# A fused attention and MoE kernel: pass two's weights split into the buffers they are first multiplied from

## The chip, the cores and the metric

The kernel runs on one core of a Trainium2 chip. The metric is device microseconds of one launch, the median of several runs. Operands and results are float32; the two weight matrices arrive as float64 and are decoded on the chip.

## What is computed

Windowed attention with a linear bias over 8 batches and 8 heads, its output laid out as 4608 tokens of 512 features, then a two-layer MLP with the activation h * erf(softplus(h)).

```python
def attention(q, k, v):                      # each (8, 8, 576, 64), window 128, scale 1/8
    scores = scale * q @ k.T
    rel = pos[:, None] - pos[None, :]
    bias = slopes[h] * -abs(rel)             # slopes 2^-(h+1), h = 0..7
    scores = where((rel >= 0) & (rel < 128), scores + bias, -1e9)
    attn = exp(scores - max); attn = attn / (sum(attn) + 1e-9)
    return attn @ v

def reference(q, k, v, moe_w_in, moe_w_out): # w_in (512, 2048), w_out (2048, 512), float64
    x = attention(q, k, v) as (4608, 512)    # 8 batches x 576 rows, 8 heads x 64
    h = x @ w_in
    sp = max(h, 0) + log1p(exp(-abs(h)))
    return ((h * erf(sp)) @ w_out).astype(float32)
```

## The kernel before

Every matmul of the MLP is made from float32r operands: a number is split into a high part (its rounding) and a low part (the rest), and high*high + high*low + low*high are summed in PSUM.

**Stages.** Attention runs over 48 pairs of heads (12 chunks of 384 tokens, 4 pairs each), and the MLP's pass one runs among it: 12 chunks by the first 6 blocks of 128 hidden columns (`NF1`), 72 units; its products are L989 (with w_in) and L1065 (with w_out). Its weights lie split in one large tile, `w1`, for the whole pass. Pass one's partial outputs go to DRAM (`pd`). Pass two takes the other 10 blocks in 5 pairs (`NP`), over 6 chunks of 768 tokens: 30 rounds `R`, round R with pair p = R mod 5. A pair's w_in product is done in Strassen's form with 7 products (L1178), of which the left operands are sums of weight blocks; then activation, then 12 products with w_out (L1217). After a chunk's fifth round, each of its 6 output tiles is made: `pd` is loaded into an output buffer `ot` (L1089), PSUM is added (L1090), and it is stored (L1095).

**Pass two's weights.** `Weights.pair` decodes two blocks of w_in (L846 to L850 on DVE, L835 and L843 on ACT), forms the sums (L888 to L891), and `split` makes high and low parts of wa, wb, wc and wd in a staging buffer `wb` of which there are two (`WB`), and sends them to DRAM (L873); the same for two blocks of w_out (we). Decoded tiles share three buffers, `wt` (`RB`), handed out in the order of the code. For every round, the first five too, `fetch` (L1119) then reads the pair back from DRAM: 14*256 columns for w_in (`wi`) and 4*512 for w_out (`wo`). `wi` has three homes in rotation: two buffers of the pool that takes over attention's memory, and for R mod 3 = 2 a place in `w1`, which pass one must first have left; `wo` has three buffers. The pool exists only once attention is done (`gone`).

**Order.** Nothing is ordered at run time. Each operation is given to a planner with its candidate engines and costs, a due time `at`, and its buffers; `Plan.run` is a list scheduler that simulates the engines with these costs and writes each engine's instruction order, in which the engine then runs, waiting on semaphores. Of the ready operations that find their buffers free, an engine takes the one due earliest. A transfer is reckoned at 380 GB/s (280 in the first 9 us) after 0.65 us and lands 1.3 us later (L391, L392). All DMAs are issued by SP, in the planner's order. Due times of the weights' pairs stand `W2A` = 40 ahead of their round's.

**Memory.** Chunks 1 and 2 of attention's output are kept in two buffers of a pool `early`, which is among attention's pools and is closed with them. There are three output buffers `ot` (`OB`).

Of the kernel before, what the change touches and what calls it, by code (L numbers as in the profile page):

```python
# [19 lines left out]
P = 128  # L20
# [21 lines left out]
PB, XB, OB, TB = 3, 3, 3, 2  # L42
WB, RB = 2, 3
# [3 lines left out]
SLOW, RATE = 9.0, 280e3  # L47
# [9 lines left out]
W2A, W2B, WL = 40, 8.0, 36  # L57
# [69 lines left out]
def passes(w, a):  # L127
# [17 lines left out]
    while out:  # L145
# [10 lines left out]
LEFT = {"A11": (0, 512), "A12": (256, 768), "S1": (1024, 1536), "S2": (1280, 1792),  # L156
        "S3": (2048, 2560), "S4": (2304, 2816), "A22": (3072, 3328)}
# [41 lines left out]
class View(Buf):  # L199
# [6 lines left out]
    @property  # L206
    def all(self):
        x = self.whole[:, self.c0 : self.c0 + self.n]
        return x.rearrange("p (k n) -> p k n", k=self.k) if self.k > 1 else x.bitcast(F32)
# [5 lines left out]
class Strip(Part):  # L215


    def __init__(self, whole, c0, n):
        super().__init__(whole)
        self.c0, self.n = c0, n  # L220

    @property
    def all(self):
        return self.whole.all.rearrange("p a n -> p (a n)")[:, self.c0 : self.c0 + self.n]
# [19 lines left out]
class Plan:  # L244
# [17 lines left out]
    def op(self, costs, emit, r=(), w=(), at=0.0, moved=0, rows=1.0):  # L262
# [19 lines left out]
        for b in [*r, *w]:  # L282
            if isinstance(b, Part):
                bufs[id(b.whole)] = b.whole
# [11 lines left out]
    def run(self):  # L296
# [55 lines left out]
        while events:  # L352
# [17 lines left out]
            for e in ("SP", "PE", "Act", "DVE", "Pool"):  # L370
                while free.get(e, 0.0) <= t + 1e-9 and ready.get(e):
# [89 lines left out]
class Attention:  # L461


    def __init__(self, tc, plan, actx, qk, vb, plain, bias, ident, moe):
# [5 lines left out]
        self.qkp, self.vp, self.pp, self.ptp, self.xsb, fixed, moe.early = (  # L470
            sb(n) for n in ("qkp", "vp", "pp", "ptp", "xsb", "tables", "early"))
# [335 lines left out]
class Weights:  # L807
# [69 lines left out]
    def pair(self, p, f, wi, wo, at):  # L877
# [16 lines left out]
        self.split(f"wa{p}", lambda: t1.all.bitcast(F32), DM, [t1], wi[0], at)  # L894
        self.split(f"wb{p}", lambda: sums[:, :2].rearrange("p a n -> p (a n)"), DM, [sums], wi[1], at)
        self.split(f"wc{p}", lambda: sums[:, 2:].rearrange("p a n -> p (a n)"), DM, [sums], wi[2], at)
        self.split(f"wd{p}", lambda: t2[:, SB:].bitcast(F32), SB, [t2], wi[3], at)
        for j in range(2):
            t = self.decode(1, f + j, at + 0.5 * W2B)
            self.split(f"we{p}_{j}", lambda t=t: t.all.bitcast(F32), DM, [t], wo[j], at + 0.5 * W2B)  # L900


class Moe:
# [4 lines left out]
    def __init__(self, tc, plan, ctx, x_dram, part_dram, out):  # L908
# [3 lines left out]
        self.xp, self.hp, self.op_ = (sb(n) for n in ("xp", "hp", "outp"))  # L912
# [3 lines left out]
        self.raw, self.direct_parts = {}, []  # L916
# [182 lines left out]
    def blocks_pass(self, wi, wo, pool, home, gone, time):  # L1099
# [17 lines left out]
    def fetch(self, src, w, over, n, gone, at):  # L1117
        nc, op = self.nc, self.plan.op
        op(emit=lambda e: nc.sync.dma_start(w.all, src[0].whole.ap), r=[*src, gone], w=[w, *over], at=at, **dma(P * n * 4))  # L1119
        return w  # L1120
# [37 lines left out]

    def pair(self, C, p, R, x, wi, wo, po, at):
# [10 lines left out]
        def product(ps, a, c, begin):  # L1170
            xh, xl = x[c]
            ah, al = LEFT[a]

            def emit(e):
                for k in range(2):
                    w = lambda o: wi[:, o + P * k : o + P * k + P].bitcast(F32R)
# [5 lines left out]
            op({"PE": 6 * f32r_us(CH) + 0.015}, emit, r=[wi, xh, xl] + [ps] * (not begin), w=[ps], at=at + MH)  # L1182
# [26 lines left out]
        for j, t in [(j, t) for t in tiles for j in range(2)] if last and not C else [(j, t) for j in range(2) for t in tiles]:  # L1209
            gh, gl = g[j]  # L1210
            if True:

                def mm(e, j=j, t=t, gh=gh, gl=gl):
                    cs = slice(P * t, P * t + P)
                    w = [wo[:, DM * (2 * j + k) : DM * (2 * j + k + 1)].bitcast(F32R) for k in range(2)]
# [6 lines left out]
                op({"PE": 3 * f32r_us(DM) + 0.015}, mm, r=[gh, gl, wo], w=[po[t]], at=at + MP)  # L1222
# [5 lines left out]
def tile_kernel(ctx, tc, qk, vb, w_in, w_out, plain, bias, out, nb=B):  # L1228
# [47 lines left out]
    ops += [o for o in plan.ops[len(ops) :] if any(b in o.bufs for b in (moe.raw[1], moe.raw[2]))]  # L1276
# [7 lines left out]
    def pieces(b, *cuts):  # L1284
        out = []
        for c0, c1 in zip(cuts, cuts[1:]):
            out.append(Buf(ap=b.ap[:, c0:c1]))
            out[-1].whole = b
        return out
# [3 lines left out]
    for p in range(NP):  # L1293
        w1.later = [attention.loaded[min(WN + p * WD, len(attention.loaded) - 1)]]
# [85 lines left out]
```

## Time and profile before

| | us |
|---|---|
| median of the 3 runs | 979.7 |
| the runs | 979.7, 967.86, 980.14 |
| the profiled execution | 977.34 |
| its span, first to last instruction | 975.6 |
| mean granted TensorE clock | 0.991 |

The span is cut into windows, and for each window the profile gives the busy time of each engine. What PE is not busy in a window is time lost by the engine that is busy nearly throughout; the lists of waits, of instructions in order of time and the chain that ended last tell what it waited for.

### The profile page before, as it was taken

How to read it: one execution, taken by the hardware profiler on the slowest of the kernel's cores; microseconds unless marked ns; L12 is line 12 of the kernel's file. 1: busy time of each engine (PE TensorE's matmuls, PEld its weight loads, DVE VectorE, ACT ScalarE, POOL GpSimd, SP SyncE). 2: the span in 40 equal slices, each digit the busy share in tenths (PEclk: the TensorE clock that was granted, in tenths of full speed). 3: DMA queues.
4: the chain of work that ended last, by engine and by line, in shares of the span. 5: the costliest groups of instructions: out<-in, count | busy, mean ns of one | idle time of the engine just before them, and what ended most of it. 6: DMA issues, size and time to landing. Idle time of an engine off the chain costs nothing.

```text
span 975.6 us, 26523 instructions
## 1 busy us (share of the span) xinstructions
PE 938.7 (96%) x11080; PEld 812.5 (83%) x11080; DVE 640.8 (66%) x1485; ACT 636.0 (65%) x1282; POOL 148.4 (15%) x295
## 2 busy tenths in 40 slices
PE   8789999999999999999999999999999999999998
PEld 7577788787888777878888898998989898889896
DVE  6888667457666668787989875565374375454433
ACT  7897767557765666776868566565665565475652
POOL 3532423232333314400000000000000000000000
PEclk9999999999999999999999999999999999999999
DMA  7764435645664486589699887666856765855711
GB/s 245 248 207 132 155 119 184 177 150 179 189 198 141 160 285 208 169 313 368 260 314 323 304 316 244 262 263 208 296 201 221 284 265 183 301 183 217 252 72 65
DMA packets 58760, 216.06 MB, mean 221 GB/s; under 512 B 6928, under 2 KB 16144, under 8 KB 50960
## 3 DMA queue, kind: packets, MB, share of 16 engines
q1 hardware_dynamic: 58640, 214.36, 63.8%
q8 instruction: 87, 1.43, 0.6%
q14 instruction: 33, 0.27, 0.1%
HBM read 171.61 MB, written 42.73 MB: 220 GB/s over the span
## 4 chain that ended last, share of the span: by engine, by line
PE 69%; DMA 12%; DVE 7%; issue 2%; POOL 2%; ACT 2%; SPq 0%; DVEq 0%; POOLq 0%; ACTq 0%
PE banks L1217 20%; PE banks L1178 16%; PE banks L1065 13%; PE banks L989 12%; PE banks L751 5%; PE banks L647 3%; DMA ot<-pd 3%; DMA out_dram<-ot 3%; DMA xr<-xd 2%; POOL p L712 2%; DMA wi<-wa 1%; DMA y<-xd 1%; DVE p L681 1%; DVE pa L729 1%; DMA wi<-wi 1%
## 5 line engine op out<-in xcount | busy, mean ns | idle before, releaser
L1217 PE MATMUL banks<-wo,gh 128*128 128x512 f32 x720 | 223.9, 392 | 2.9 <-DVE ot L1090 2.9
L971 ACT COPY hs<-banks 128x384 f32<-128x384 f32 x143 | 68.3, 478 | 173.5 <-PE banks L1178 136.0
L712 POOL TENSOR_SCALAR p<-p,st 128x160 f32<-128x160 f32 (+2 forms) x282 | 141.3, 520 | 262.3 <-DVE st L704 231.4
L989 PE MATMUL banks<-xh,w 128*128 128x384 f32 x576 | 170.4, 350 | 3.7 <-ACT hs L971 2.0
L1217 PEld LDWEIGHTS banks<-wo,gh 128*128 128x128 f32 x720 | 133.1, 188 | 24.9 <-DVE ot L1090 4.5
L1065 PE MATMUL banks<-w,gh 128*128 128x512 f32 x432 | 141.8, 409 | 3.4 <-ACT ot L971 2.2
L1217 PE MATMUL banks<-wo,gl 128*128 128x512 f32 x360 | 141.7, 394 | 0.0
L689 ACT ACTIVATE p<-p,st 128x160 f32<-128x160 f32 (+2 forms) x288 | 120.3, 421 | 30.5 <-DVE st L681 30.4
L989 PEld LDWEIGHTS banks<-xh,w 128*128 128x128 f32 x576 | 107.2, 190 | 15.5 <-ACT hs L971 6.7
L1044 DVE TENSOR_TENSOR hs<-s,hs 128x768 f32<-128x768 f32 (+1 forms) x103 | 90.1, 902 | 29.5 <-ACT s L1034 29.5
L681 DVE CUSTOM_DVE_ANT_0 p<-banks,tables 128x160 f32<-128x160 f32 (+2 forms) x288 | 75.8, 318 | 42.6 <-PE banks L647 41.7
L989 PE MATMUL banks<-xl,w 128*128 128x384 f32 x288 | 97.9, 340 | 0.0
L1189 DVE TENSOR_TENSOR hs<-banks,hs 128x384 f32<-128x384 f32 x90 | 49.9, 555 | 72.2 <-PE banks L1178 43.3
L1065 PEld LDWEIGHTS banks<-w,gh 128*128 128x128 f32 x432 | 77.8, 191 | 23.1 <-issue 6.2
L1178 PE MATMUL banks<-w,wi 128*128 128x384 f32 x480 | 94.9, 337 | 1.3 <-DVE hs L1189 1.3
L1048 DVE TENSOR_TENSOR gl<-hs,gh 128x768 fp32r<-128x768 f32 (+1 forms) x103 | 91.8, 910 | 3.8 <-ACT gh L971 2.3
L1178 PEld LDWEIGHTS banks<-w,wi 128*128 128x128 f32 x480 | 85.2, 188 | 6.2 <-DVE hs L1189 1.6
L1065 PE MATMUL banks<-w,gl 128*128 128x512 f32 x216 | 86.5, 400 | 0.0
L1032 ACT ACTIVATE s<-hs 128x768 f32<-128x768 f32 (+1 forms) x103 | 76.2, 794 | 13.2 <-DVE hs L1189 12.9
L1217 PEld LDWEIGHTS banks<-wo,gl 128*128 128x128 f32 x360 | 67.5, 188 | 14.3
L1034 ACT ACTIVATE s<-s 128x768 f32<-128x768 f32 (+1 forms) x103 | 76.2, 794 | 0.5
L751 PEld LDWEIGHTS banks<-pa,v 32*64 32x64 f32 x4576 | 59.1, 132 | 19.2 <-issue 8.2
(112 smaller groups left out, 1418.0 us busy)
## 6 DMA issues: line engine op xcount, KB each, us to landing
wi<-wi SPq DMA_DIRECT2D x20, 1792.0 KB, 8.0
wo<-wo SPq DMA_DIRECT2D x30, 1024.0 KB, 7.4
w<-wi SPq DMA_DIRECT2D x10, 1792.0 KB, 7.4
v<-v_b SPq DMA_DIRECT2D x24, 512.0 KB, 4.0
qk<-qk SPq DMA_DIRECT2D x24, 400.0 KB, 4.0
pd<-ot SPq DMA_DIRECT2D x36, 256.0 KB, 3.9
y<-xd SPq DMA_DIRECT2D x12, 768.0 KB, 6.1
wri<-w_in SPq DMA_DIRECT2D x16, 512.0 KB, 5.2
```

Source lines behind the costliest of these rows:

```text
L681: nc.vector.tensor_tensor_reduce(out=dst(j), in0=cut(ps[j].all), in1=cut(table[:, half * j + c0 : half * j + c0 + n]), scale=-0.125, scala ...
L689: nc.scalar.activation(dst(j), dst(j), AF.Exp, bias=low[:, j : j + 1], scale=-1.0, accum_out=total[:, j : j + 1])
L712: (nc.vector if e == "DVE" else nc.gpsimd).tensor_scalar(dst, dst, totals[t][:, j : j + 1], 1.0, op0=ALU.mult, op1=ALU.mult)
L751: nc.tensor.matmul(whole[64 * j : 64 * j + 64, first + a, 32 * t0 : 32 * (t0 + n)], lhsT=y.v[rows, 128 * slot + 64 * j : 128 * slot + 64 * ...
L989: nc.tensor.matmul(ps[:, :W], lhsT=ww[:, cs], rhs=xx[:, k], start=(k2 + k + n == 0), stop=(k2 + k + n == 4),)
L1032: A.activation(s[:, :n], hs[:, :n], AF.Softplus)
L1034: A.activation(s[:, :n], s[:, :n], AF.Erf)
L1044: op({"DVE": dve(n)}, lambda e, s=s, hs=hs, n=n: V.tensor_tensor(hs[:, :n], s[:, :n], hs[:, :n], ALU.mult), r=[s, *own], w=[hs], at=at)
L1048: op({"DVE": dve(n)}, lambda e, gh=gh, gl=gl, hs=hs, n=n: V.tensor_tensor(gl[:, :n], hs[:, :n], gh[:, :n], SUB), r=[hs, gh], w=[gl], at=at)
L1065: nc.tensor.matmul(po.all, lhsT=gg[:, cs], rhs=w.all, start=(u["start"] and n == 0), stop=(u["end"] and n == 2),)
L1178: nc.tensor.matmul(ps[:, :CH], lhsT=w(o), rhs=y[:, k], start=(begin and k + n == 0), stop=(k + n == 3), skip_group_check=not begin)
L1217: nc.tensor.matmul(po[t].all, lhsT=gg[:, cs], rhs=w[k], start=(first and j + n == 0), stop=(last and j + n == 3),)
```

## The change

`split` now writes the high and low parts into the buffer from which the pair's first round multiplies (`own`, one of the three homes of `wi`, or a `wo` buffer), and sends them to DRAM from there. The first five rounds fetch nothing; the later 25 fetch as before. The staging buffers `wb` are gone. The homes of `wi` are now one buffer in `early` (tag `e`, shared with chunks 1 and 2 of attention's output), one in the pool after attention, and the place in `w1`. `early` is opened with the MLP's pools and lasts to the end. A product depends on the one part of the weights that it reads (`CUTS`) instead of on the whole fetch. Because a split writes the home itself, the splits of pair 1 and all w_out splits now come after attention is done, those of pair 2 after pass one has left its place in `w1`, those of pairs 3 and 4 after the rounds 0 and 1 have used their buffers; the w_out splits of pairs 3 and 4 after the w_out products of rounds 0 and 1.

There are five output buffers instead of three. The planner reckons transfers at 330 GB/s instead of 380 and 2.2 us to land instead of 1.3; `W2A` is 30 instead of 40.

```diff
-PB, XB, OB, TB = 3, 3, 3, 2
-WB, RB = 2, 3
+PB, XB, OB, TB = 3, 3, 5, 2
+RB = 3
 QB, VB = 4, 2
 
 TURN, TS = 0.32, 0.0
-SLOW, RATE = 9.0, 280e3
+SLOW, RATE, RATE2, LAG = 9.0, 280e3, 330e3, 2.2
...
-W2A, W2B, WL = 40, 8.0, 36
+W2A, W2B, WL = 30, 8.0, 36
...
+CUTS = (0, 1024, 2048, 3072, 3584)
+LEFT = {"A11": (0, 0, 512), "A12": (0, 256, 768), "S1": (1, 1024, 1536), "S2": (1, 1280, 1792),
+        "S3": (2, 2048, 2560), "S4": (2, 2304, 2816), "A22": (3, 3072, 3328)}
...
-                        transfer = max(transfer, best.end + 0.65) + best.moved / (380e3 if transfer > SLOW else RATE)
-                        best.lag = transfer + 1.3 - best.end
+                        transfer = max(transfer, best.end + 0.65) + best.moved / (RATE2 if transfer > SLOW else RATE)
+                        best.lag = transfer + LAG - best.end
...
-    def split(self, name, src, n, r, to, at):
+    def split(self, src, n, r, own, over, to, at):
 
         nc, op = self.nc, self.plan.op
-        wb = Buf(self.stage, [P, 2, DM], F32R, "wb", WB, name)
         op({"Act": act(n), "DVE": dve(n, True), "Pool": pool_cast(n)},
-           lambda e: Moe.copy(self, e, wb[:, 0, :n], src()), r=r, w=[wb], at=at)
-        op({"DVE": dve(n)}, lambda e: nc.vector.tensor_tensor(wb[:, 1, :n], src(), wb[:, 0, :n], SUB),
-           r=[*r, wb], w=[wb], at=at)
-        op(emit=lambda e: nc.sync.dma_start(
-            to.ap.rearrange("p (two n) -> p two n", two=2), wb[:, :, :n].bitcast(F32)),
-           r=[wb], w=[to], at=at, **dma(2 * P * n * 4))
-
-    def pair(self, p, f, wi, wo, at):
+           lambda e: Moe.copy(self, e, own.all[:, :n], src()), r=r, w=[own, *over], at=at)
+        op({"DVE": dve(n)}, lambda e: nc.vector.tensor_tensor(own.all[:, n:], src(), own.all[:, :n], SUB),
+           r=[*r, own], w=[own], at=at)
+        op(emit=lambda e: nc.sync.dma_start(to.ap, own.all.bitcast(F32)), r=[own], w=[to], at=at, **dma(2 * P * n * 4))
+
+    def pair(self, p, f, wi, wo, own, at):
 
         nc, op = self.nc, self.plan.op
...
+        (wa, wb, wc, wd), over, need = own[0]
+        self.split(lambda: t1.all.bitcast(F32), DM, [t1, *need], wa, over, wi[0], at)
+        self.split(lambda: sums[:, :2].rearrange("p a n -> p (a n)"), DM, [sums, *need], wb, over, wi[1], at)
+        self.split(lambda: sums[:, 2:].rearrange("p a n -> p (a n)"), DM, [sums, *need], wc, over, wi[2], at)
+        self.split(lambda: t2[:, SB:].bitcast(F32), SB, [t2, *need], wd, over, wi[3], at)
         for j in range(2):
             t = self.decode(1, f + j, at + 0.5 * W2B)
...
             t = self.decode(1, f + j, at + 0.5 * W2B)
-            self.split(f"we{p}_{j}", lambda t=t: t.all.bitcast(F32), DM, [t], wo[j], at + 0.5 * W2B)
+            self.split(lambda t=t: t.all.bitcast(F32), DM, [t, *own[2]], own[1][j], [], wo[j], at + 0.5 * W2B)
...
-            pool, tag = (self.early, f"xr{c}") if c in (1, 2) else (self.xp, "xr")
-            self.raw[c] = Buf(pool, [P, NK, CH], F32, tag, 1, f"xr{c}")
+            if c in (1, 2):
+                self.both = self.both or Buf(self.early, [P, 14 * SB], F32, "e", 1, "xr12")
+                self.raw[c] = Strip(self.both, (c - 1) * NK * CH, NK * CH, NK)
+            else:
+                self.raw[c] = Buf(self.xp, [P, NK, CH], F32, "xr", 1, f"xr{c}")
...
-                own, over = home["wi"] if R % 3 == 2 else (Buf(pool, [P, 14 * SB], F32, "wi", 2, f"wi{R}"), [])
-                a = self.fetch(wi[p], own, over * (R == 2), 14 * SB, gone, time(R) - WL)
-                own = Buf(pool, [P, 4 * DM], F32, "wo", 3, f"wo{R}")
-                b = self.fetch(wo[p], own, [], 4 * DM, gone, time(R) - WL + 0.6 * TR)
+                if R < NP:
+                    a, b = mine[p][0][0], mine[p][1]
+                else:
+                    dst = self.wi_home(R, F32, home, pool)
+                    a = self.fetch(wi[p], dst[1], gone, time(R) - WL, dst[0])
+                    dst = Buf(pool, [P, 4 * DM], F32, "wo", 3, f"wo{R}")
+                    b = self.fetch(wo[p], [dst], gone, time(R) - WL + 0.6 * TR, dst)
                 self.pair(C, p, R, x, a, b, po, time(R))
...
+    def wi_home(self, R, dtype, home, pool):
+
+        if R % 3 == 2:
+            return home["w1"], home["parts"], home["wi"] * (R == 2)
+        own = Buf(self.early, [P, 14 * SB], dtype, "e", 1, f"wi{R}") if R % 3 == 0 else Buf(pool, [P, 14 * SB], dtype, "wi", 1, f"wi{R}")
+        return own, [Strip(own, c0, c1 - c0) for c0, c1 in zip(CUTS, CUTS[1:])], []
...
-            op({"PE": 6 * f32r_us(CH) + 0.015}, emit, r=[wi, xh, xl] + [ps] * (not begin), w=[ps], at=at + MH)
+            op({"PE": 6 * f32r_us(CH) + 0.015}, emit, r=[own, xh, xl] + [ps] * (not begin), w=[ps], at=at + MH)
...
-                op({"PE": 3 * f32r_us(DM) + 0.015}, mm, r=[gh, gl, wo], w=[po[t]], at=at + MP)
+                op({"PE": 3 * f32r_us(DM) + 0.015}, mm, r=[gh, gl, wp], w=[po[t]], at=at + MP)
...
-    ops += [o for o in plan.ops[len(ops) :] if any(b in o.bufs for b in (moe.raw[1], moe.raw[2]))]
...
+    mine = []
+    for p in range(NP):
+        dst = moe.wi_home(p, F32R, home, pool2)
+        out = Buf(pool2, [P, 4 * DM], F32R, "wo", 3, f"wo{p}")
+        mine.append(((dst[1], dst[2], [gone] * (p % 3 == 1)), [Strip(out, 2 * j * DM, 2 * DM) for j in range(2)], [gone]))
+        w1.later = [attention.loaded[min(WN + p * WD, len(attention.loaded) - 1)]]
+        w1.pair(p, NF1 + 2 * p, wi[p], wo[p], mine[p], t1 + p * TR - W2A)
+    moe.blocks_pass(wi, wo, mine, pool2, home, gone, lambda R: t1 + R * TR)
     plan.run()
```

## Rows read from the trace of the kernel before

**Rows 1.** The page: the span, and each engine's busy time, share and instructions.
```profile
span 975.6 us, 26523 instructions
...
PE 938.7 (96%) x11080; PEld 812.5 (83%) x11080; DVE 640.8 (66%) x1485; ACT 636.0 (65%) x1282; POOL 148.4 (15%) x295
```

**Rows 2.** Busy by window: length, PE, PEld, DVE, ACT, POOL, TensorE clock, DMA share, GB/s.
```profile
0.00:120.00 120.00, 103.60 (x2005) 85.77 (x2005) 97.08 (x329) 96.44 (x277) 48.67 (x91) 0.97 0.62 198
...
120.00:420.00 300.00, 290.33 (x6388) 241.60 (x6389) 203.26 (x658) 199.14 (x563) 95.72 (x201) 0.98 0.57 179
...
420.00:440.00 20.00, 17.63 (x87) 15.07 (x86) 15.84 (x26) 16.06 (x24) 1.09 (x1) 1.00 0.97 363
...
480.00:540.00 60.00, 58.40 (x286) 51.14 (x286) 56.70 (x95) 44.57 (x62) 1.81 (x2) 1.00 0.91 329
...
600.00:950.00 350.00, 347.10 (x1729) 312.08 (x1728) 179.92 (x247) 208.58 (x268) 0.00 (x0) 1.00 0.64 229
```

**Rows 3.** Waits of PE over the span: us in total, times, longest.
```profile
PE banks L1065 <- ACT ot L971: 2.2, 1, 2.2
...
PE banks L1178 <- DVE hs L1189: 1.6, 2, 1.3
...
PE banks L1217 <- DVE ot L1090: 2.9, 5, 0.9
```

**Rows 4.** ACT's instructions around 433 us: start, duration, tile, idle time before.
```profile
432.77 0.66 ACT L843 ACTIVATE wuo<-wro 128x512 int32<-128x512 uint32 x1
...
433.90 0.83 ACT L971 CAST xh<-xr 128x768 fp32r<-128x768 f32 x1 [0.47 <-DMA xr<-xd]
...
435.38 1.55 ACT L971 COPY ot<-banks 128x512 f32<-128x512 f32 x3
```

**Rows 5.** DVE's instructions that waited for a staging buffer's transfer.
```profile
442.64 0.29 DVE L975 CAST wd<-wti 128x256 fp32r<-128x256 f32 x1 [3.52 <-DMA wi<-wb]
...
506.55 0.43 DVE L975 CAST wc<-ws 128x512 fp32r<-128x512 f32 x1 [1.84 <-DMA wi<-wa]
...
539.95 0.43 DVE L975 CAST wc<-ws 128x512 fp32r<-128x512 f32 x1 [0.20 <-DMA wi<-wa]
```

**Rows 6.** The chain that ended last, at the start of pass two: start, duration.
```profile
475.01 2.21 PE banks L989 x12
...
478.61 2.08 PE banks L1178 x12
...
544.67 7.72 DMA wi<-wi
...
552.53 2.35 PE banks L1178 x12
```

**Rows 7.** The same chain at the second chunk boundary of pass two.
```profile
674.32 6.66 DMA ot<-pd
...
681.75 5.73 PE banks L1217 x24
```

**Rows 8.** DMA issues: count, KB of one, median us from issue to landing.
```profile
wi<-wi SPq DMA_DIRECT2D x20, 1792.0 KB, 8.0
...
wo<-wo SPq DMA_DIRECT2D x30, 1024.0 KB, 7.4
...
w<-wi SPq DMA_DIRECT2D x10, 1792.0 KB, 7.4
```

**Rows 9.** Busy by 2 us windows in pass one, columns as in Rows 2.
```profile
326.00:328.00 2.00, 0.92 (x54) 0.75 (x59) 2.00 (x14) 1.99 (x9) 0.00 (x0) 1.00 0.02 6
...
330.00:332.00 2.00, 2.00 (x7) 1.60 (x5) 1.73 (x5) 1.14 (x4) 0.46 (x1) 0.50 0.75 249
```

**Rows 10.** DVE's and SP's instructions around the last pair of weights.
```profile
521.80 0.42 DVE L846 TENSOR_SCALAR wti<-wqi 128x512 int32<-128x512 int32 x1
...
528.51 0.32 SPq L1119 DMA_DIRECT2D wo<-wo  x1
...
541.88 0.42 DVE L871 TENSOR_TENSOR wd<-wti,wd 128x256 fp32r<-128x256 f32 x1
```

More of the change, by code (lines that the diff above doesn't have):

```diff
@@ L215, with __init__ @@
 class Strip(Part):
-    def __init__(self, whole, c0, n):
+    def __init__(self, whole, c0, n, k=1):
         super().__init__(whole)
-        self.c0, self.n = c0, n
+        self.c0, self.n, self.k = c0, n, k
     @property
     def all(self):
-        return self.whole.all.rearrange("p a n -> p (a n)")[:, self.c0 : self.c0 + self.n]
+        x = self.whole.all
+        x = (x.rearrange("p a n -> p (a n)") if len(self.whole.shape) > 2 else x)[:, self.c0 : self.c0 + self.n]
+        return x.rearrange("p (k n) -> p k n", k=self.k) if self.k > 1 else x
 class Banks:
@@ L911, in __init__ @@
         sb = lambda name: ctx.enter_context(tc.tile_pool(name=name, bufs=1))
-        self.xp, self.hp, self.op_ = (sb(n) for n in ("xp", "hp", "outp"))
+        self.xp, self.hp, self.op_, self.early = (sb(n) for n in ("xp", "hp", "outp", "early"))
         self.ps = Banks(tc, ctx)
@@ L1097, in store, with blocks_pass @@
             op(emit=rows, r=[ot], at=at, **dma(nbytes, len(rows_of(T))))
-    def blocks_pass(self, wi, wo, pool, home, gone, time):
+    def blocks_pass(self, wi, wo, mine, pool, home, gone, time):
         nc, op = self.nc, self.plan.op
@@ L1109, in blocks_pass, with fetch, read @@
             for p in range(NP):
-                own, over = home["wi"] if R % 3 == 2 else (Buf(pool, [P, 14 * SB], F32, "wi", 2, f"wi{R}"), [])
-                a = self.fetch(wi[p], own, over * (R == 2), 14 * SB, gone, time(R) - WL)
-                own = Buf(pool, [P, 4 * DM], F32, "wo", 3, f"wo{R}")
-                b = self.fetch(wo[p], own, [], 4 * DM, gone, time(R) - WL + 0.6 * TR)
+                if R < NP:
[5 more added lines that the diff above has]
+                    b = self.fetch(wo[p], [dst], gone, time(R) - WL + 0.6 * TR, dst)
                 self.pair(C, p, R, x, a, b, po, time(R))
                 R += 1
-    def fetch(self, src, w, over, n, gone, at):
-        nc, op = self.nc, self.plan.op
-        op(emit=lambda e: nc.sync.dma_start(w.all, src[0].whole.ap), r=[*src, gone], w=[w, *over], at=at, **dma(P * n * 4))
-        return w
+    def wi_home(self, R, dtype, home, pool):
[3 more added lines that the diff above has]
+        return own, [Strip(own, c0, c1 - c0) for c0, c1 in zip(CUTS, CUTS[1:])], []
+    def fetch(self, src, parts, gone, at, w):
+        nc, op = self.nc, self.plan.op
+        n = src[0].whole.n
+        def read(e):
+            x = w.all
+            nc.sync.dma_start(x if x.dtype == F32 else x.bitcast(F32), src[0].whole.ap)
+        op(emit=read, r=[*src, gone], w=parts, at=at, **dma(P * n * 4))
+        return parts
     def load_blocks(self, C, begun, at, pool, home, gone):
@@ L1157, in load_blocks, with f32r @@
         return x
+    def f32r(self, x):
+        return x if x.dtype == F32R else x.bitcast(F32R)
     def pair(self, C, p, R, x, wi, wo, po, at):
@@ L1211, in pair, with mm @@
             if True:
-                def mm(e, j=j, t=t, gh=gh, gl=gl):
+                wp, c0 = (wo[j], 0) if len(wo) == 2 else (wo[0], 2 * DM * j)
+                def mm(e, j=j, t=t, gh=gh, gl=gl, wp=wp, c0=c0):
                     cs = slice(P * t, P * t + P)
-                    w = [wo[:, DM * (2 * j + k) : DM * (2 * j + k + 1)].bitcast(F32R) for k in range(2)]
+                    w = [self.f32r(wp.all[:, c0 + DM * k : c0 + DM * k + DM]) for k in range(2)]
                     for n, (gg, k) in enumerate(((gh, 0), (gh, 1), (gl, 0))):
@@ L1288, in pieces @@
             out[-1].whole = b
+            b.n = cuts[-1]
         return out
@@ L1292, in tile_kernel @@
     wo = [pieces(b, 0, 1024, 2048) for b in drams[1]]
-    for p in range(NP):
-        w1.later = [attention.loaded[min(WN + p * WD, len(attention.loaded) - 1)]]
-        w1.pair(p, NF1 + 2 * p, wi[p], wo[p], t1 + p * TR - W2A)
-    home, c0 = {}, 0
+    home = {"w1": View(whole, 0, 14 * SB), "parts": [View(whole, c0, c1 - c0) for c0, c1 in zip(CUTS, CUTS[1:])]}
+    c0 = 0
     for name, n, k in (("wi", 14 * SB, 1), ("T1", 2 * CH, 2), ("T3", 2 * CH, 2), ("B22", 2 * CH, 2), ("T4", 2 * CH, 2)):
@@ L1301, in tile_kernel @@
         c1 = c0 + n * k
-        home[name] = *views, [slots[j] for j in range(c0 // DM, (c1 - 1) // DM + 1)]
+        over = [slots[j] for j in range(c0 // DM, (c1 - 1) // DM + 1)]
+        home[name] = over if name == "wi" else (*views, over)
         c0 = c1
-    moe.blocks_pass(wi, wo, pool2, home, gone, lambda R: t1 + R * TR)
+    mine = []
[6 more added lines that the diff above has]
+    moe.blocks_pass(wi, wo, mine, pool2, home, gone, lambda R: t1 + R * TR)
     plan.run()
```

24 lines of the change are left out of this document (10 added, 14 removed).

## The prediction

> **What bounds the kernel now.** I read the page first: PE is busy for 938.7 of 975.6 us, 96%; DVE and ACT have 66% and 65% [rows 1]. So time comes only from two places: the 37 us in which PE is idle, and the stretches in which it runs at the lower clock. Next, the busy time by window, to see where these lie [rows 2]. From 0 to 120 us PE misses 16.4 us and from 120 to 420 us 9.7 us, both with a mean clock below 1.00: this is attention with pass one. From 420 to 440 us it misses 2.4 us, from 480 to 540 us 1.6 us, and in the 350 us of pass two from 600 to 950 us only 2.9 us. DMA is near full where pass two begins (share 0.97, 363 GB/s) and at 0.64 in pass two. Then PE's waits, which name what ended last [rows 3]: one wait of 2.2 us for the copy of an output accumulator, 1.6 us in two waits for the sums of Strassen's products, and 2.9 us in five waits for an output tile at the five chunk boundaries. These 6.7 us are all that the change can reach outside pass one.
>
> **The first five rounds fetch nothing.** Of the 60 fetches, five of 1792 KB and five of 1024 KB go [rows 8]. That is 14.4 MB; at 363 GB/s, 40 us of transfer, off SP's queue too. Splits, sums, stores to DRAM and matmuls keep their number and shapes, so engine work is unchanged.
>
> What does it do for PE? The 2.2 us wait near 434 us goes back to ACT: a weight conversion at 432.77, then the cast of a chunk of attention's output at 433.90, whose load had kept ACT idle 0.47 us, then other casts, and the accumulator copies only at 435.38 [rows 4]. The fetches left at 426 us, beside that load. The least gain is that 0.47, the most the whole 2.2 us. I take 1.1: the cast can go when the weight conversion begins (433.90 to 432.77), as that conversion is due 10 later by `W2A` and can yield. The casts ahead of the copies remain, so it lies nearer to the lower end.
>
> In that window the granted clock is 1.00 in spite of the gap [rows 2], so I give no clock back here. The Trainium skill, "TensorE: Matmul & The Clock Gate", section "HAM oscillation — how this bites in real kernels", says that gaps in PE's work can bring its clock down and make the next matmuls slow; by it this gap's removal might return about another 1 us. The row shows no such fall behind this gap, so the rule gets nothing here.
>
> The fetch of the fifth round lands at 552.4 and its first product starts at 552.53 [rows 6]: it is on the chain, but PE still had w_out products, so its removal is worth 0 by itself. It opens 7.7 us of room.
>
> **No staging buffer.** DVE waited four times for a `wb` buffer whose transfer crawled; three are shown, of 3.52, 1.84 and 0.20 us [rows 5]. The first cost PE nothing that is seen in its waits. Behind that of 1.84 us at 506.55, with DVE busy for 56.7 of 60 us [rows 2], lie the two waits of PE for sums, 1.6 us [rows 3]. A DVE that is so full has nothing to absorb the wait with. Bounds 0 and 1.6; I take 1.6, because the removed wait is larger than the loss.
>
> **The waits added.** A split now waits for its home, and what stands behind it on DVE or ACT (the reading of PSUM, gh, gl) waits too, and PE for that. Pair 0 goes into `early`, whose chunks 1 and 2 are long used. Pair 2 needs pass one's w_in, last used at 477.2, two rounds before its own; a round takes (552.53 - 478.61) / 4 = 18.5 us here [rows 6]. The tightest is pair 4. Round 0's `wo` buffer comes free where the next fetch into it left, 528.5; pair 3's w_out splits wait for it, and as `wt` has three buffers, pair 4 can't be decoded before. Its decoding began at 521.80 and its last split at 541.88, 20.5 us with that split [rows 10]. From 528.5, with 2.5 us for the two w_out splits ahead (0.43 a cast [rows 5], and a subtraction at twice the 0.42 of half the columns [rows 10]), it ends at 551.5: 1 us before the product at 552.53. The fetch that is saved covers the late start. I take 0; if cover is gone, PE pays what exceeds 1 us. One row bounds such a wait: 3.52 us, for each of the releases by rounds 0 and 1 (two w_in buffers, two w_out buffers), 14.1 us at most.
>
> **Five output buffers.** At a boundary six tiles share three buffers, so the fourth load waits for the first store: the load ran from 674.32 to 681.0, and PE went on at 681.75 after the addition [rows 7]. Five times this, 2.9 us, at most 0.9 each [rows 3]. With five buffers only the sixth tile takes that route. It lands no later than the fourth does today, and its accumulator is wanted two tiles later: 5.73 us for 24 matmuls is 0.72 for a tile's three, so 1.4 us, more than 0.9. All 2.9 us go. Bounds 0 (if SP, in which these loads stand in order with the weights' fetches, is late anyway) and 2.9.
>
> **The planner's reckoning.** It re-deals every engine's order, pass one's above all. For 1792 KB the old figures give 0.65 + 4.83 + 1.3 = 6.8 us and the new 0.65 + 5.56 + 2.2 = 8.4; measured were 8.0 and 7.4. For 1024 KB, 4.7 and 6.0 against 7.4 [rows 8]. The new ones are closer on two of three and nowhere short of the largest by over 1.4 us. A load that lands after its planned time stops an engine that executes in order. One such stall stands in pass one at 326 us: PE busy for 0.92 of 2 us, then a window at clock 0.50 [rows 9], 1.08 + 1.0 = 2.1 us. I count half of that as won, 1.0, since the order around it will be another one. The bounds come from the idle time before 420 us, 26 us [rows 2]: a re-dealt order might win or lose a third, 8 us either way.
>
> The Trainium skill, "DMA: Bandwidth & Descriptors", section "Anatomy of one DMA — SWDGE (gpsimd) path", speaks against these figures: about 2.0 us plus the bytes at 436 GB/s, an estimate of 6.2 us for 1792 KB. The measured 7.4 to 8.0 us decide against it for these transfers. By the page the planner would now hold work back without need, and the sum would lose its last term: 971.7.
>
> **The sum** is made against the profiled execution, 977.3 us, 1.7 more than its span. 977.3 - 1.1 - 1.6 - 2.9 - 1.0 = 970.7. Two of the runs shown lie above that execution by 2.4 and 2.8 us and one 9.5 below, so I leave the sum where it is; the median of before, 979.7, is the measure for faster or slower.
>
> **Rivals.**
> 1. *Hidden anyway.* At pass two's start DVE stays 95% busy; the waits move to other instructions and only the boundaries gain. For it: the same DVE work in the same window. Against: 5.6 us of shown DVE waits vanish. 977.3 - 2.9 = 974.4.
> 2. *Held splits, slower.* Round 0 and 1's releases come late for the planned order, and DVE, full, passes it on to PE. For it: 1 us of margin for pair 4. Against: planned order includes these waits. At the full price 970.7 + 1.6 (the removed wait replaced by these) + 14.1 = 986.4; it decides from 6.6 us of passed-on wait, where all gains are used up.
> 3. *Pass one re-dealt for the worse.* The larger reckoning holds loads' readers back, or moves new gaps in: 970.7 + 8 = 978.7, no change. This is the outcome that the quoted rule on transfers points to; the measured landing times speak against it.
> 4. *Pass one re-dealt for the better*, late loads no longer stop DVE and ACT: 970.7 - 8 = 962.7. With a favourable draw of the runs it passes 2%.
> 5. *The change doesn't do what it says*: the splits move behind the fetch's old time, so no earlier start. Its time is that of rival 1, with which it goes.
>
> **Chances.** The forecast 0.50 with its own range of 966 to 975; rival 1 0.17; rival 2 0.08; rival 3 0.12; rival 4 0.13. The range of 8 in 10 leaves out rival 2's upper half and rival 4's lower: 960 to 980. About 2% is what a measurement of this kernel can tell from no change; that is 960.1 below and 999 above. Faster by over 2%: most of rival 4's lower half and a little of the forecast's, 0.11. Slower by over 2%: 0.02, as even rival 2's full price stays under 999. Within 2%: 0.87.
>
> **What would show it.** Right: issues of `wi`, `w` and `wo` fetches fall from 60 to 50; no DVE wait for a weight's transfer; the five waits of L1217 for `ot` gone; PE idle in the transition under 1.5 us. Wrong: a new wait of DVE or ACT on PE ahead of a split around rounds 2 to 4; PE's idle time before 420 us off by over 8 us from 26.

## The result, and the profile after

The changed kernel takes 959.83 us (median of 6 runs, 958.78 to 962.83); the kernel before took 975.91 us in the same comparison (6 runs, 967.86 to 980.14). The ratio is 0.9847 with a 95% interval of 0.9801 to 0.9893: faster, though by less than 2%. The forecast was 970.7, so the direction was right and the gain nearly twice what was forecast: 16.1 us against 9.0 (979.7 - 970.7). The median lies 0.2 us under the lower end of the range of 960 to 980, and 6 us under the forecast's own range of 966 to 975.

The kernel before varies from one execution to the next: its medians in all the comparisons here are 971.5 to 975.9 us, so its profiled execution of 977.34 us lies at the slow end, and 1 to 6 of the 18 us between the two profiles are that execution's own.

The page of the changed kernel, the span and the engines' busy time, against [rows 1]:

```profile
span 957.5 us, 26479 instructions
...
PE 934.9 (98%) x11080; PEld 812.3 (85%) x11080; DVE 631.8 (66%) x1471; ACT 642.3 (67%) x1298; POOL 154.9 (16%) x293
```

PE executes the same 11080 matmuls. Its idle time fell from 36.9 to 22.6 us and its busy time by 3.8 us, which makes the 18.1 us of the span. The windows tell where, columns as in [rows 2]:

```profile
0.00:120.00 120.00, 105.90 (x1982) 88.53 (x1982) 96.41 (x331) 93.81 (x274) 48.43 (x87) 0.93 0.61 194
120.00:420.00 300.00, 297.42 (x6467) 248.37 (x6467) 207.69 (x664) 210.19 (x578) 103.64 (x204) 1.00 0.61 187
420.00:440.00 20.00, 20.00 (x102) 18.04 (x101) 18.08 (x31) 16.41 (x26) 0.86 (x1) 1.00 0.86 307
480.00:540.00 60.00, 59.30 (x297) 52.30 (x296) 55.94 (x95) 49.43 (x70) 2.00 (x2) 1.00 0.76 267
600.00:950.00 350.00, 348.38 (x1728) 312.59 (x1727) 178.96 (x245) 205.98 (x263) 0.00 (x0) 1.00 0.59 214
```

From 120 to 420 us PE misses 2.6 us instead of 9.7, and the granted clock there rose from 0.98 to 1.00; that is the largest part. The first 120 us give 2.3 us of idle time back at a lower clock (0.93 against 0.97), the transition from 420 to 600 us 3.5, pass two's boundaries 1.3. PE's waits answer to [rows 3]:

```profile
PE banks L994 <- ACT hs L976: 1.7, 1, 1.7
PE banks L1244 <- DVE ot L1095: 1.6, 1, 1.6
...
PE banks L1203 <- DVE hs L980: 0.3, 1, 0.3
```

(L1203 is the w_in product of pass two, L1244 the w_out product, L1095 the addition at a boundary: L1178, L1217 and L1090 of before.) The 2.2 us near 434 us is gone, the waits for Strassen's sums are gone (0.3 us for the copy of a product is left), and one wait at a chunk boundary is left of five. The first product of pass two, in the instructions of its line (shortest, median and longest ns; first and last start), begins at 464.2 instead of 478.4:

```profile
L1203 PE MATMUL banks<-yh,wi x240: 331/334/441, 464.2 to 909.8; 128*128 128x384 f32 x120
```

So 14 of the 18 us are won before pass two has begun. The DMA issues show the promised removal, 50 fetches instead of 60 [rows 8]:

```profile
wi<-wi SPq DMA_DIRECT2D x16, 1792.0 KB, 7.9
wo<-wo SPq DMA_DIRECT2D x25, 1024.0 KB, 5.7
w<-wi SPq DMA_DIRECT2D x9, 1792.0 KB, 7.5
```

### The profile page after: what moved, and what is told of

Its sections match the earlier page's. It is cut to its first block, busy times and chain, and to the rows that moved or that the text cites. A ratio compares the mean times of both kernels' runs of the same rounds, so it can differ in the third digit from the quotient of the medians.

```text
span 957.5 us, 26479 instructions
## 1 busy us (share of the span) xinstructions
PE 934.9 (98%) x11080; PEld 812.3 (85%) x11080; DVE 631.8 (66%) x1471; ACT 642.3 (67%) x1298; POOL 154.9 (16%) x293
## 4 chain that ended last, share of the span: by engine, by line
PE 55%; ACT 1%; DMA 1%; DVE 1%; SPq 0%; POOL 0%; issue 0%; DVEq 0%
PE banks L1244 25%; PE banks L1203 22%; PE banks L1070 5%; PE banks L994 3%; DMA ot<-pd 1%; SPq L1100 0%; POOL p L716 0%; DVE gl L1053 0%; ACT s L1039 0%; ACT s L1037 0%; PE banks L755 0%; DVE ot L1095 0%; ACT L1039 0%; ACT L1037 0%; DVE pa L733 0%; ACT wi L976 0%
## 5 line engine op out<-in xcount | busy, mean ns | idle before, releaser
L1244 PE MATMUL banks<-wo,gh 128*128 128x512 f32 x720 | 223.5, 391 | 1.6 <-DVE ot L1095 1.6
L976 ACT COPY hs<-banks 128x384 f32<-128x384 f32 x155 | 74.2, 479 | 178.9 <-PE banks L1203 143.9
L716 POOL TENSOR_SCALAR p<-p,st 128x160 f32<-128x160 f32 (+2 forms) x278 | 147.1, 550 | 249.7 <-DVE st L708 200.9
L1244 PEld LDWEIGHTS banks<-wo,gh 128*128 128x128 f32 x720 | 133.3, 188 | 22.9 <-DVE ot L1095 2.4
L1244 PE MATMUL banks<-wo,gl 128*128 128x512 f32 x360 | 141.7, 394 | 0.0
L1070 PE MATMUL banks<-w,gh 128*128 128x512 f32 x432 | 139.6, 404 | 0.0
L1203 PE MATMUL banks<-w,wi 128*128 128x384 f32 x480 | 94.1, 336 | 0.0
L1070 PEld LDWEIGHTS banks<-w,gh 128*128 128x128 f32 x432 | 77.0, 188 | 18.1 <-issue 5.8
L1203 PEld LDWEIGHTS banks<-w,wi 128*128 128x128 f32 x480 | 84.8, 188 | 4.6 <-DVE hs L980 0.3
L1244 PEld LDWEIGHTS banks<-wo,gl 128*128 128x128 f32 x360 | 67.5, 187 | 14.4
L755 PEld LDWEIGHTS banks<-pa,v 32*64 32x64 f32 x4576 | 58.9, 132 | 16.7 <-issue 6.6
```

What stands on the lines that cost most here:

```text
L716: (nc.vector if e == "DVE" else nc.gpsimd).tensor_scalar(dst, dst, totals[t][:, j : j + 1], 1.0, op0=ALU.mult, op1=ALU.mult)
L976: self.nc.scalar.copy(out, src)
L1070: nc.tensor.matmul(po.all, lhsT=gg[:, cs], rhs=w.all, start=(u["start"] and n == 0), stop=(u["end"] and n == 2),)
L1203: nc.tensor.matmul(ps[:, :CH], lhsT=w(o), rhs=y[:, k], start=(begin and k + n == 0), stop=(k + n == 3), skip_group_check=not begin)
L1244: nc.tensor.matmul(po[t].all, lhsT=gg[:, cs], rhs=w[k], start=(first and j + n == 0), stop=(last and j + n == 3),)
```

## The experiments

Three theories for where the gain comes from: the direct split and the buffers bring it; the planner's reckoning does, through another order in pass one; or neither alone, since the one makes room that the other takes up. Each ratio is against runs of the kernel before in the same comparison, with its 95% interval. In the table below, idle time of PE is the window's length less PE's busy time, from one profiled execution of each.

### One part of the change at a time

**e1_reckon**: the kernel before with the new reckoning alone.

```diff
-... best.moved / (380e3 if transfer > SLOW else RATE)
-best.lag = transfer + 1.3 - best.end
+... best.moved / (330e3 if transfer > SLOW else RATE)
+best.lag = transfer + 2.2 - best.end
```

> The kernel before with only the planner's reckoning changed (330 GB/s, 2.2 us to land). Theory A, the reckoning re-dealt pass one so that DVE and ACT no longer stand before late transfers, and that is most of the 16 us: about 966 us, PE idle from 120 to 420 us under 5 us instead of 9.7, waits of DVE and ACT for transfers nearly gone. Theory B, the direct splits and the missing fetches are the cause: within 3 us of before, about 976, pass one as before. Theory C, any new order moves the time by chance: anywhere from 968 to 984, with new stalls in other places.

Measured: 969.48 us, 0.9957 (0.9936 to 0.9977).

**e6_reckon_w2a**: the same, and the weights due 10 later.

```diff
-W2A, W2B, WL = 40, 8.0, 36
+W2A, W2B, WL = 30, 8.0, 36
```

> The kernel before with the new reckoning and the weights' due time 30 ahead instead of 40: everything but the direct split and the output buffers. Theory A: about 966, as e1. Theory B: about 976. What is left between this run and e4_ob3 is the direct split alone: 1 to 3 us by the prediction's terms for fetches and staging.

Measured: 968.39 us, 0.9954 (0.9930 to 0.9977).

**e2_undo_reckon**: the changed kernel with the old reckoning; splits, buffers and `W2A` stay changed.

```diff
-SLOW, RATE, RATE2, LAG = 9.0, 280e3, 330e3, 2.2
+SLOW, RATE, RATE2, LAG = 9.0, 280e3, 380e3, 1.3
```

> The changed kernel with the old reckoning (380 GB/s, 1.3 us to land). Theory A: about 969 us, the waits of DVE and ACT for transfers of pass one come back, and PE idle from 120 to 420 us is again over 7 us. Theory B: about 960, no change. Theory C: anywhere from 955 to 972.

Measured: 974.87 us, 1.0026 (0.9998 to 1.0053).

**e4_ob3**: the changed kernel with three output buffers.

```diff
-PB, XB, OB, TB = 3, 3, 5, 2
+PB, XB, OB, TB = 3, 3, 3, 2
```

> The changed kernel with three output buffers. By the prediction's term the five boundary waits of the w_out products come back, 2.9 us in place of the 1.6 us that are left: about 961 to 962.5 us, all of it after 600 us. If the buffers matter in pass one too (its partial outputs use them), PE idle before 420 us grows as well and the time passes 963.

Measured: 959.62 us, 0.9884 (0.9843 to 0.9925).

PE's idle time by stage, in us:

| kernel | 0-120 | 120-420 | 420-480 | 480-600 | 600-940 | span |
|---|---|---|---|---|---|---|
| before | 16.4 | 9.7 | 2.4 | 1.8 | 2.9 | 975.6 |
| after | 14.1 | 2.6 | 0 | 0.7 | 1.6 | 957.5 |
| e1 | 13.9 | 3.5 | 0 | 8.4 | 0.2 | 968.5 |
| e6 | 15.0 | 3.8 | 0 | 5.9 | 0.7 | 965.5 |
| e2 | 14.5 | 8.9 | 1.8 | 1.7 | 4.2 | 971.2 |
| e4 | 15.0 | 3.3 | 0 | 0.7 | 0 | 954.6 |

Neither half makes the gain. Split and buffers without the reckoning (e2) are worth nothing; the reckoning without them (e1, e6) less than half a per cent; together, with three buffers, 1.2%. That is the third theory, and the table shows how. It was formed on these results: the expectations had chance as their third theory, and e2's 974.87 us lies outside what any of the three gave it. The new reckoning empties pass one of idle time whether or not the split is changed (3.5, 3.8 and 3.3 us against 8.9 and 9.7), and pass two begins at 466.6 in e1. But there the kernel before loses most of it again. Three rows of e1, from the order of time of PE and of SP's queue (start, duration; in brackets the idle time before and what ended it):

```profile
540.06 1.14 SPq L1119 DMA_DIRECT2D wi<-wi  x2
546.29 1.22 PE L1217 MATMUL banks<-wo,gh 128*128 128x512 f32 x2 [5.90 <-ACT gh L971]
548.36 0.55 PE L1178 MATMUL banks<-yh,wi 128*128 128x384 f32 x1
```

The fetch of the fifth pair can be issued only after the pair's last split has gone to DRAM, at 540.06; the next w_in product starts at 548.36. In between PE has run out of the w_out products that covered this fetch before [rows 6], and waits for the activation of the last round. In e1 the activation's chain and this fetch, which lands 8.1 us after its issue, end within half a microsecond of each other. In e6 the chain that ended last goes through the transfer itself (SP's store of the last split, the fetch, the first product):

```profile
539.20 0.32 SPq L873
...
539.68 7.95 DMA wi<-wi
547.63 0.04 issue
547.68 1.40 PE banks L1178 x6
```

The granted clock falls in this gap as well: it is 0.74 from 540 to 550 us in e1 and 0.66 in e6, against 1.00 there in before, after and e4, and PE is busy 4.7 us longer in e6 than in e4 (936.3, 931.6).

So the removal of this trip to DRAM and back is worth next to nothing at the pace of the kernel before (480 to 600 us: 1.8 to 1.7 with the old reckoning), and 5 to 8 us of idle time when pass two begins 12 us earlier while the last split of the weights goes out only 5 us earlier (537.3 against 542.3): 5.9 and 8.4 down to 0.7. e4 and e6 differ by the direct split, with its homes and parts, alone. Their medians lie 8.8 us apart, where the expectation had 1 to 3, and their intervals don't overlap. A new order alone can move the time by nearly as much (e11 below), so it is these rows, not the difference by itself, that show the cause.

The same runs correct the account of the chunk boundaries. Windows of e2 and of e4 over pass two:

```profile
600.00:940.00 340.00, 335.83 (x1667) 302.31 (x1666) 176.27 (x241) 201.79 (x260) 0.00 (x0) 0.99 0.63 227
```

```profile
600.00:940.00 340.00, 340.00 (x1692) 305.96 (x1691) 177.34 (x242) 205.40 (x262) 0.00 (x0) 1.00 0.62 222
```

With five buffers and the old reckoning 4.2 us are lost, with three and the new one nothing. The five waits for `ot` do vanish in e2, but other waits stand in their place. Its waits of PE in this stretch are one row, and DVE's and PE's instructions at the second boundary show what it is:

```profile
PE banks L1203 <- DVE hs L1214: 4.2, 3, 1.9
```

```profile
672.57 0.69 DVE L1095 TENSOR_TENSOR ot<-banks,ot 128x512 f32<-128x512 f32 x1 [4.91 <-DMA out_dram<-ot]
673.17 0.55 DVE L1214 TENSOR_TENSOR hs<-banks,hs 128x384 f32<-128x384 f32 x1
```

```profile
673.77 1.31 PE L1203 MATMUL banks<-w,wi 128*128 128x384 f32 x6 [1.52 <-DVE hs L1214]
```

DVE stood 4.91 us at one tile's addition (at the next boundary 5.30 us), and behind it in DVE's order stood the sum of Strassen's products that PE needed. SP's queue shows why the tile was late: its load is the sixth, and goes out behind the eleven stores of the five tiles before it. (The bracket names a store; the load landed at 672.5 us, just ahead of the addition.)

```profile
660.51 7.72 SPq L1100 DMA_DIRECT2D out_dram<-ot  x11
668.28 0.58 SPq L1094 DMA_DIRECT2D ot<-pd  x1
```

In e4 no such addition stands longer than this one, 2.09 us, and PE loses nothing there:

```profile
740.86 0.69 DVE L1095 TENSOR_TENSOR ot<-banks,ot 128x512 f32<-128x512 f32 x1 [2.09 <-DMA ot<-pd]
```

So under the new reckoning three buffers are enough. Five output buffers on the kernel before weren't tried.

### Which of the two figures

Theories: the time to land decides, since a transfer's readers wait for it; or the late loads of attention's chunks do, which stop DVE and ACT in pass one; or any change of the figures merely deals another order, better or worse.

**e7_lag_only** (380 GB/s, 2.2 us) and **e8_rate_only** (330 GB/s, 1.3 us), on the changed kernel.

```diff
-SLOW, RATE, RATE2, LAG = 9.0, 280e3, 330e3, 2.2
+SLOW, RATE, RATE2, LAG = 9.0, 280e3, 380e3, 2.2
```

```diff
-SLOW, RATE, RATE2, LAG = 9.0, 280e3, 330e3, 2.2
+SLOW, RATE, RATE2, LAG = 9.0, 280e3, 330e3, 1.3
```

> The changed kernel with the landing time at 2.2 us but the rate back at 380 GB/s. Theory A1, what hurts pass one is that small transfers (192 to 768 KB) are reckoned to land about 1 us early, a fixed error: nearly all of the reckoning's gain stays, about 960 to 962 us, and no waits of DVE or ACT for attention's chunks in pass one. Theory C, a new order is luck: anywhere from 955 to 972.

> The changed kernel with the rate at 330 GB/s but the landing time back at 1.3 us. Theory A1: about 969 us; a slower rate adds 0.3 us to a transfer of 768 KB and under 0.1 to one of 192 KB, so the waits for attention's chunks stay. Theory A2, the rate and its backlog matter: about 961.

Measured: e7 964.02 us, 0.9914 (0.9885 to 0.9943); e8 959.28 us, 0.9862 (0.9828 to 0.9897). Each takes PE's idle time from 120 to 420 us down (4.9 and 3.7 us, against e2's 8.9). The rate alone brings the full gain, the time to land more than half of it: the first theory falls.

**e9_chunk_only**: new figures for the stores and loads of attention's chunks alone, old ones for all other transfers.

```diff
-... (RATE2 if transfer > SLOW else RATE)
-best.lag = transfer + LAG - best.end
+... ((RATE2 if best.late else 380e3) if transfer > SLOW else RATE)
+best.lag = transfer + (LAG if best.late else 1.3) - best.end
```

> The changed kernel with the old reckoning (380 GB/s, 1.3 us) for all transfers but two kinds: the stores of attention's output to DRAM and its loads as pass one's chunks, which keep 330 GB/s and 2.2 us. Theory A3, the late chunk of attention's output is what stops DVE, ACT and then PE in pass one: about 962, pass one as in the changed kernel, only boundary waits back. If the other loads' lateness (queries, keys, values, weights) does it: about 970.

Measured: 971.97 us, 1.0000 (0.9976 to 1.0024). Waits for chunk loads in e2, the kernel it differs from, from 120 to 420 us (total us, times, longest):

```profile
DVE xh L980 <- DMA xr<-xd: 5.4, 3, 3.2
...
ACT xh L976 <- DMA xr<-xd: 3.2, 1, 3.2
```

In e9 there are none, and of waits of DVE and ACT for any transfer only one of 0.4 us. PE still misses 7.0 us of 300 there (e2: 8.9), and the time is that of the kernel before. e7 and e8, which miss less, have 6.8 and 5.5 us of such waits in this stretch. So the second theory falls, for other late loads too: most of these waits were hidden.

**e11_near** (340 GB/s, 2.0 us) and **e12_over** (310 GB/s, 2.8 us): smaller and larger steps in the same direction.

```diff
-SLOW, RATE, RATE2, LAG = 9.0, 280e3, 330e3, 2.2
+SLOW, RATE, RATE2, LAG = 9.0, 280e3, 340e3, 2.0
```

```diff
-SLOW, RATE, RATE2, LAG = 9.0, 280e3, 330e3, 2.2
+SLOW, RATE, RATE2, LAG = 9.0, 280e3, 310e3, 2.8
```

> The changed kernel with a reckoning nearby: 340 GB/s and 2.0 us. Theory A: within 3 us of the changed kernel, 957 to 963, because the order is again free of late transfers. Theory C, the order's luck: more than 4 us away in either direction.

> The changed kernel with a still slower reckoning, 310 GB/s and 2.8 us. Theory D: from 120 to 420 us under 5 us idle, from 480 to 600 us under 2 us, no boundary waits; the first 120 us by luck, 18 to 36 us lost: 953 to 970 us. If an overstated landing time holds work back, as the quoted fit of transfer times would have it: idle time from 120 to 420 us over 6 us.

Measured: e11 967.15 us, 0.9946 (0.9919 to 0.9973); e12 970.53 us, 0.9963 (0.9935 to 0.9991). The gain doesn't follow the figures in one direction. e11 keeps pass one's gain (3.4 us idle from 120 to 420) and loses it at the start, where its window shows 8.3 us less of PE than that of after, at a lower clock:

```profile
0.00:120.00 120.00, 97.57 (x1976) 81.57 (x1977) 91.98 (x328) 94.74 (x276) 49.20 (x89) 0.89 0.62 194
```

Most of it is three waits for ACT's copies of pass one's products, against 2.1 us in the same line of e14 below:

```profile
PE banks L994 <- ACT hs L976: 8.3, 3, 5.8
```

e12 has a start like that of after (14.0 us idle) and loses pass one (9.0). That is the third theory, in part: the order's particulars matter by as much as the figures.

### The start kept, the rest re-dealt

A theory from this: two stages decide independently, so the old figures for the first 100 us and the new ones behind should add the better of both.

**e13_switch** (then 330 GB/s, 2.2 us) and **e14_switch_near** (then 340 GB/s, 2.0 us).

```diff
-best.lag = transfer + LAG - best.end
+begun = transfer
+... (RATE if begun <= SLOW else 380e3 if begun <= TURN2 else RATE2)
+best.lag = transfer + (1.3 if begun <= TURN2 else LAG) - best.end
```

> The changed kernel with the old reckoning for the planner's first 100 us and the new one after. Theory D, the gain has two parts: from 120 us on the new reckoning removes stalls whatever its exact figures, while the first 120 us go by the order's luck. In the runs so far, idle time plus time lost to the clock from 0 to 120 us was 18 us with the old reckoning and 23 with the new one, so about 955 us here, with 0 to 120 us as in the run with the old reckoning and under 5 us of idle time from 120 to 420 us. If the new reckoning is needed from the start: 965 or more.

> As e13_switch, but with 340 GB/s and 2.0 us after the first 100 us, the figures that from the start gave 967 us. Theory D: those 967 us came from the first 120 us alone, where 36 us were lost to idle time and clock; with the old start's 18 us the time is 950 to 954 us. Theory C, 340 and 2.0 make a worse order throughout: 960 to 967.

Measured: e13 961.14 us, 0.9874 (0.9830 to 0.9917); e14 959.00 us, 0.9857 (0.9821 to 0.9893). The start of e14, against e11's row above:

```profile
0.00:120.00 120.00, 104.41 (x2002) 87.21 (x2005) 96.25 (x329) 94.93 (x275) 46.99 (x89) 0.97 0.62 194
```

PE's idle time there is 6.8 us less than in e11, and the span 7.7 us less (964.3 to 956.6): stages do add. But both expectations are missed, by 5 to 6 us, and neither run comes below the changed kernel beyond the intervals, since its own start has as little idle time (14.1 us). No run here clearly beats the changed kernel. The lower clock that the start of after shows costs less than its size suggests: between e11 and e14 the mean clock's difference would be worth (0.97 - 0.89) * 120 = 9.6 us, and the spans leave 1 for it.

**e5_w2a40**: the changed kernel with the old due time of the weights.

```diff
-W2A, W2B, WL = 30, 8.0, 36
+W2A, W2B, WL = 40, 8.0, 36
```

> The changed kernel with the weights' due time 40 ahead again instead of 30. By the prediction the due time is worth at most 1 us: 958 to 962 us, with idle time from 480 to 600 us under 2 us. If the weights' earlier place crowds pass one: over 965, with idle time from 340 to 480 us.

Measured: 964.31 us, 0.9916 (0.9890 to 0.9941), against 0.9847 (0.9801 to 0.9893) with 30. Its idle time from 480 to 600 us is 3.1 us instead of 0.7 (the profile is of the fastest of its ten executions, 960.69 us). The intervals, of two comparisons, just touch; on the kernel before the due time made no difference (e1 and e6). A gain of a few us is likely, not shown.

### Where pass one's idle time went

From 120 to 420 us, the profile names for most of the lost time no other engine: "issue". PE's waits of this stretch, for before, after and e2, the rows with that word:

```profile
PE banks L647 <- issue: 6.2, 4, 2.1
PE banks L751 <- issue: 2.0, 5, 0.6
```

```profile
PE banks L755 <- issue: 1.1, 1, 1.1
PE banks L651 <- issue: 0.6, 2, 0.4
```

```profile
PE banks L651 <- issue: 4.4, 4, 1.6
PE banks L755 <- issue: 1.9, 3, 0.8
PE banks L1070 <- issue: 0.2, 1, 0.2
```

8.2 us in nine waits before, of which 1.3 lie ahead of 120 us, and 1.7 in three after: 5.2 of the 7.1 us that this stretch won. The others: e9 7.0, e13 4.4, e12 4.1, e8 3.6, e6 3.4, e4 3.2, e1 2.8, e14 2.3, e5 and e11 2.1, e7 1.6. In before and after all fall into the streams of attention's small products (L647 and L751, L651 and L755 in after), where PE goes through dozens of instructions in a few us. Two of before's, in order of time, and the 1 us windows of the first:

```profile
351.29 0.48 PE L647 MATMUL banks<-qk 64*32 64x160 f32 x8 [2.13 <-issue]
...
386.67 0.46 PE L647 MATMUL banks<-qk 64*32 64x160 f32 x4 [1.97 <-issue]
```

```profile
349.00:350.00 1.00, 0.16 (x8) 0.00 (x0) 0.00 (x0) 0.00 (x0) 0.14 (x1) 1.00 0.58 78
350.00:351.00 1.00, 0.00 (x0) 0.00 (x0) 0.00 (x0) 0.00 (x0) 0.00 (x0) 1.00 0.81 305
```

PE, DVE and ACT stand still together while DMA moves data. The DMA queues name a candidate. In the list of queues (packets, MB, share), before's whole span has 87 transfers on an instruction queue, and from 348 to 352 us one of them runs:

```profile
q8 instruction: 87, 1.43, 0.6%
...
q8 instruction: 1, 0.02, 1.4%
```

87 for PE's 22160 instructions (matmuls and weight loads) is one of 16 KB for every 255. Lined up by the trace's packet records, all nine waits of before end 2.3 to 2.5 us after the start of one such transfer, and the DMA share in the 3 us ahead of the nine transfers is 0.78 to 1.01, against a mean of 0.59 ahead of all 51 in this stretch. In all fourteen kernels the waits of this kind between 118 and 420 us end 2.2 to 3.3 us after the start of such a transfer. The sixteen longer than 1 us have a share of 0.81 or more ahead of it; seven have one under 0.05, and none of these lasts over 0.7 us. So PE seems to wait here for its own instructions, where it uses them up fast, and long where the DMA engines are full. That is a coincidence in time, and no run isolates it. Why the new orders meet it less often stays open: the mean share ahead of all 52 is no lower in after (0.65).

In before the granted clock falls to 0.50, the lower of its two levels (1.2 and 2.4 GHz), three times in this stretch: behind the wait of 1.8 us that ends at 120.5, behind the stall at 326 us [rows 9], and behind the second of the two waits above; behind the first, the longest, it doesn't fall. Windows in the first and the last of the three falls, columns as in [rows 2]:

```profile
122.00:124.00 2.00, 2.00 (x6) 1.60 (x5) 2.00 (x10) 1.99 (x3) 0.00 (x0) 0.50 0.66 203
388.00:390.00 2.00, 2.00 (x6) 1.63 (x5) 2.00 (x8) 1.77 (x10) 0.00 (x0) 0.50 0.54 145
```

In after it doesn't fall in this stretch. But it falls more in the first 120 us, and the mean over the whole span is 0.991 in both, so no gain of the clock over the kernel is shown.

The Trainium skill, "Runtime: NRT & Kernel Launch", section "Instruction fetch mechanics", says that an engine fetches its next block of instructions by its own DMA queue while it executes, and that crossing a block is mostly hidden. Most are hidden here too; nine, by this reading, are not, and cost up to 2.1 us each.

## Why the prediction was right and wrong, point by point

**Fewer fetches.** The count fell as said, 60 to 50. PE's loss from 420 to 440 us went from 2.4 to 0, more than the 1.1 taken. But the missing transfers aren't needed for it: e1 keeps every fetch and loses nothing there. e2, which drops them, loses nothing from 420 to 440 us either, and 1.7 us in a new wait for DVE between 460 and 480 us. A new order alone does it. The statement that the fetch of the fifth round is worth 0 by itself, because PE still had w_out products, was right for the pace of before (e2) and wrong for that of the changed kernel: with pass two 12 us earlier it is on the chain (e6), in a stretch that loses 5.9 to 8.4 us (e1, e6). The terms were added as if none changed the others.

**No staging buffer.** Taken at 1.6; at the old pace 0.2 (e2), as rival 1 had it. The DVE waits for `wb` vanished and PE didn't notice.

**The waits added.** Taken at 0 for PE, and near 0: its idle time from 480 to 600 us is 0.7 us in after. One such wait did stand: DVE waited 2.66 us at 513.42 for round 0's w_out products, ahead of pair 3's w_out split, and PE lost nothing by it:

```profile
513.42 0.43 DVE L980 CAST wo<-wto 128x512 fp32r<-128x512 f32 x1 [2.66 <-PE banks L1244]
```

Rival 2 didn't come, though pass two begins 14 us earlier and its margin for pair 4 was put at 1 us; the planner had the waits in its order.

**Five output buffers.** Taken at 2.9, all of the five waits. Measured 1.3, and not by the buffers: they go as well with three (e1 0.2, e4 0). The step that failed is that the sixth tile "lands no later" and is wanted later. It looked at PE's accumulator alone and not at what stands behind the addition on DVE. The one boundary wait left in after shows that "lands no later" fails too: the sixth tile's load went out at 739.70 behind thirteen stores and landed 16.4 us after the chunk's first addition, where the fourth of before [rows 7] landed 13.6 us after it; and here PE waited for the accumulator itself, 1.6 us. In the chain that ended last:

```profile
739.70 5.81 DMA ot<-pd
...
745.53 0.70 DVE ot L1095
...
746.28 1.88 PE banks L1244 x7
```

**The reckoning.** The term that was mis-sized: 1.0 forecast. PE's idle time before 420 us fell from 26.1 to 16.7, by 9.4 us, beyond the bound of 8 on either side. The step that failed was to price it from the one stall at 326 us [rows 9], and to take half of that. That stall waited for DVE, 1.1 us; the waits that made up the stretch were nine others, 8.2 us, that the list of waits puts down to "issue", and the prediction doesn't mention them. The bound came from the right place (idle time by window) but a third of it was a choice, with no row behind it. And the reason given, loads that land later than planned, fits the boundaries (4.2 us from 600 to 940 us in e2 and 3.7 in e9, against 1.6 in after, though one new figure alone leaves 4.6 in e7 and 3.0 in e8), but not pass one (e9).

**The sum.** 18.0 us were won between the two profiled executions, 977.34 and 959.32, where the sum had 6.6: 9.4 before 420 us, 3.5 from 420 to 600, 1.3 behind it, and 3.8 of busy time. The three terms outside pass one made 5.6 of the sum and came to 4.8, so their total was about right for reasons that were mostly wrong. Rival 4 (962.7, chance 0.13) comes nearest in time and place, and its stated mechanism, late loads that stop DVE and ACT, is the one that e9 speaks against: no late load is left there, and PE misses 7.0 us all the same. So its nearness is luck. Rival 3 is seen in e12: a larger reckoning still, and pass one's idle time is back at 9.0 us, of which 4.1 are "issue" and most of the rest waits for DVE.

**What would show it.** Of the four signs for right, three came: the fetches, no wait of DVE for a weight's transfer, and the idle time of the transition (0.7, under 1.5 us); the five waits for `ot` became one. Both signs for wrong came: DVE's wait ahead of pair 3's split, which cost PE nothing, and over 8 us from 26 before 420 us.

## What to carry to other kernels

Where a planner writes every engine's order, its figures for transfers are a part of the kernel, as much as its buffers: here the changed kernel took 959 to 975 us between settings of 310 to 380 GB/s and 1.3 to 2.8 us, and not in one direction, so an edit should be measured at the figures that it will run with. Price a removed round trip at the pace at which the work in front of it will then run: a transfer that is covered today may be the next bound when that work ends 12 us sooner. And where an engine executes in order, ask of every late buffer what stands behind the instruction that waits for it, not only who wants that instruction's result.

## What the runs showed of the hardware

Not expected: the waits for nothing that the profile names, 0.25 to 2.1 us long, in streams of small matmuls, that end 2.3 to 2.5 us after a 16 KB transfer on the instruction queue has begun (9 of 9 in the kernel before, 8.2 us from 118 to 420 us). The granted clock fell behind some such gaps and not behind others of the same size: behind 1.1, 1.8 and 2.0 us in before, and not behind 2.1 and 2.2. And fetches of one size differ in time by far more than either figure of the planner: three of 1792 KB issued in e1 between 500 and 560 us took 8.1, 12.6 and 12.9 us, the first two of these issued 0.4 us apart, against a median of 7.9 over the span of after.
